# Moving the weight-side units, two banks, two loads and the weight sums of an attention + bilinear kernel

## The chip, the cores and the metric

The kernel runs on one core of one Trainium2 chip. The metric is the device time of one execution in microseconds (us): the median of three runs, which lay between 521.59 and 522.47. All numbers are float32; "hi" and "lo" below are a float32 number split into a part that the TensorE multiplies exactly (type fp32r) and its remainder.

## The reference

Per batch (8 of them) and head (8), two small attentions between 512 tokens `x` and 32 state rows; their outputs, put side by side over the heads, go through a bilinear layer:

```
scores  = x @ state.T / 8;   a  = softmax(scores)  over the 32 states;  xread = a  @ state   # 512 rows
scores2 = state @ x.T / 8;   a2 = softmax(scores2) over the 512 tokens; sread = a2 @ x       # 32 rows
X = concat(xread, sread), heads side by side           # 8 x (512 + 32) rows of 512
out = ((X @ w1) * (X @ w2)) @ w3 @ w_out               # w1, w2: 512x1024, w3: 1024x1024, w_out: 1024x512
```

## The kernel before

A prologue (to about 67 us) loads the weights, which come as float64, and computes w3 @ w_out once (`wo`, in hi and lo). Then it goes batch by batch.

*Stage 1* of a batch does not form xread. It multiplies the state of the batch into w1 and w2 (four *units* of w, `sw_steps`: each unit is 8 small matmuls, in the trace 16 instructions, of the line L147 into a two-bank PSUM tile, a copy `sw_hi` on ScalarE and a subtraction `sw_lo` on VectorE) and then multiplies the softmax `at` with the result (`stage1_sums`, L310). For each of 8 column groups `ft` this takes 12 matmuls into a two-bank tile; the two banks, one from w1 and one from w2, are multiplied on VectorE to give the hidden rows `g`.

*Stage 2* multiplies `g` with `wo`. Batches 0 and 1 do it token tile by token tile (`stage2`, L324, 24 matmuls for each of four tiles). Batches 2 to 7 (`fast_batch`) cut both operands into halves and use the scheme in which 7 products of halves stand for 8 (`stage2_quarters`, each product 24 matmuls of the line L427). It needs sums of quarters of `g` (VectorE) and sums of quarters of `wo`. The latter are made once, in batch 1, by four calls of `combine_weights`: for each, two sums, four differences and a split into `t_hi` and `t_lo`.

Called from inside stage 2 is the preparation of the next batch: its units of w (`side`), the end of its softmax (`at_hi`, `at_lo`), and the transposed `e` (L228) that 16 small DMAs move into place (`move_blocks`, L171). In the middle of stage 1, after the fourth group, PE runs `read_state` (L243), which makes sread of this batch from the tokens `x_s` and the moved `e`, and the scores of the next batch from `x_d`. After that the loads of the next tokens (`load_tokens`) and of the `x_d` after the next (`load_x`) are issued; each of these two tiles has one buffer.

Orders: PE and SP (the queue of all loads and small moves) run in the order in which the program is written. The order on ScalarE (ACT) and VectorE (DVE) is set by a scheduler. Every engine runs its queue in order. Each DMA has one of eight semaphores, and its issue waits until the previous DMA of that semaphore has landed.

PSUM: `two_banks()` takes one of three two-bank tiles in turn (`ps_2`, shown as `ps`), `bank()` one of two single banks (`ps_o`). A taker waits until the last reader of the buffer's former content is done. In `stage2_quarters` products 1 and 3 go to `bank_a`, 2 and 4 to `bank_e`, 5 and 6 to the two halves of one two-bank tile `pair`, 7 to `bank_f`; DVE adds them (L437).

Of the kernel before, what the change touches and what calls it, by code (L numbers as in the profile page):

```python
# [39 lines left out]
def attn_bilinear_kernel(  # L40
# [11 lines left out]
    B, _, NT, H, D = x_s.shape  # L52
# [35 lines left out]
    def bank():  # L88
        return ps_o.tile([P, NF], F32, name="ps_o")

    def two_banks():
        return ps_2.tile([P, 2, NF], F32, name="ps_2")
# [48 lines left out]
    def per_head(ps, b, moving):  # L141


        for j in range(NP):
            for q in range(KT):
                rows = slice(q * D, (q + 1) * D)
                nc.tensor.matmul(  # L147
                    ps[j * NS:(j + 1) * NS, q], sts[b][rows, j], moving(rows, j), start=True, stop=True
                )

    def load_x(b):
        sts[b] = att.tile([P, NP, NS], F32, name="st")
        nc.sync.dma_start(out=sts[b], in_=st[b])
        x_tiles[b] = att.tile([P, NP, S], F32, name="x_d", bufs=1)
        nc.sync.dma_start(out=x_tiles[b], in_=x_d[b])

    def load_tokens(b):
        token_tiles[b] = att.tile([P, NT, H, D], F32, name="x_s", bufs=1)
        nc.sync.dma_start(out=token_tiles[b], in_=x_s[b])
# [101 lines left out]
    def sw_pair():  # L261
        return [main.tile([P, KT, NF], F32R, name=f"sw_{part}", bufs=2 * HALF) for part in ("hi", "lo")]

    def sw_steps(b):
        sw_tiles.setdefault(b, {})

        def unit(half, i):
            ps = two_banks()
            as_q = ps.rearrange("p k (c f) -> p k c f", c=2)
            per_head(as_q, b, lambda rows, j: w_sb[rows, 2 * half:2 * half + 2, i, j])  # L270
            sw_tiles[b][half, i] = sw_pair()
            split(*sw_tiles[b][half, i], ps)

        return [(lambda half=half, i=i: unit(half, i)) for half in range(HALF) for i in range(2)]
# [66 lines left out]
    reads = {}  # L341

    def side_steps(b):


        if b == B:
            return [[reads[b - 1]], [], [], []]
        scores, reads[b], a2 = attention_steps(b)
        w = sw_steps(b)
        softmax = scores()  # L350
        first = partial(islice, softmax, 3)
        if b == 1:
            def rest():

                with tc.issue_after(stored[0].ins):
                    yield from softmax

            return [[first], [reads[0], w[0], w[1]], [], [rest], [w[2], w[3]], []]

        product = partial(islice, softmax, 1)  # L360
        return [[w[0], w[1], product, reads[b - 1], w[2], w[3], lambda: softmax], [], [], []]

    QF = FT // 2
    HT, HO = S // 2, DO // 2
# [1 line left out]
    def combine_weights(k):  # L366

        raw = [tmp_tile() for _ in range(2)]
        for i, whole in enumerate(raw):
            nc.vector.tensor_tensor(  # L370
                out=whole, in0=wo["hi"][:, i * QF + k].bitcast(F32), in1=wo["lo"][:, i * QF + k].bitcast(F32), op=ALU.add
            )
        b11, b12, b21, b22 = (whole[:, half * HO:(half + 1) * HO] for whole in raw for half in range(2))
        t = late.tile([P, QF, HO], F32, name="r22")
        for j, (x, y) in enumerate(((b12, b11), (b22, t[:, 0]), (b22, b12), (b21, t[:, 1]))):
            nc.vector.tensor_tensor(out=t[:, j], in0=x, in1=y, op=ALU.subtract)
        split(t_parts["hi"][:, :, k], t_parts["lo"][:, :, k], t)

    def tmp_tile():
        return main.tile([P, NF], F32, name="tmp", bufs=4)  # L380
# [40 lines left out]
    def product(ps, a, w, fresh):  # L421

        for k in range(QF):
            hi, lo = (t[:, k % 2] for t in a[k // 2])
            for n, (g, part) in enumerate(((hi, "lo"), (hi, "hi"), (lo, "hi"))):
                for tt in range(2):
                    nc.tensor.matmul(  # L427
                        ps[:, tt * HO:(tt + 1) * HO], g[:, tt * P:(tt + 1) * P], w(part, k),
                        start=(fresh and k == 0 and n == 0 and tt == 0), stop=(k == QF - 1 and n == 2),
                        skip_group_check=True,  # L430
                    )

    def stage2_quarters(b, q, side):
        half = lambda o: slice(o * HO, (o + 1) * HO)
        b_part = lambda i, o: (lambda part, k: wo[part][:, i * QF + k, half(o)])
        t_part = lambda j: (lambda part, k: t_parts[part][:, j, k])
        sum2 = lambda out, x, y: nc.vector.tensor_tensor(out=out, in0=x, in1=y, op=ALU.add)  # L437
        c11, c21, m7, m1 = (tmp_tile() for _ in range(4))

        def stored_quarter(o, rows, cols):  # L440
            for tt in range(2):
                first = (2 * rows + tt) * P
                nc.scalar.dma_start(out=out[b, first:first + P, half(cols)], in_=o[:, half(tt)])

        bank_a = bank()
        product(bank_a, q["a11"], b_part(0, 0), True)
        nc.scalar.copy(out=m1, in_=bank_a)
        bank_e = bank()
        product(bank_e, q["s3"], t_part(2), True)
        nc.scalar.copy(out=m7, in_=bank_e)  # L450
        a22 = quarter_pairs()
        for i in range(2):
            split(*a22[i], q["r22"][:, 2 * i:2 * i + 2])
        side()
        product(bank_a, q["a12"], b_part(1, 0), False)
        nc.scalar.copy(out=c11, in_=bank_a)
        stored_quarter(c11, 0, 0)
        s2 = quarter_pairs()
        s = [raw[:, :, 0:HT] for raw in q["raw"]]
        for i in range(2):  # L460
            split(*s2[i], s[i])
        product(bank_e, a22, t_part(3), False)
        for i in range(2):
            hi, lo = (t.bitcast(F32) for t in q["a12"][i])
            nc.vector.tensor_tensor(out=s[i], in0=hi, in1=s[i], op=ALU.subtract)
            nc.vector.tensor_tensor(out=s[i], in0=lo, in1=s[i], op=ALU.add)
        s1 = quarter_pairs()
        for i in range(2):
            split(*s1[i], q["raw"][i][:, :, HT:S])
        pair = two_banks()  # L470
        product(pair[:, 0], s2, t_part(1), True)
        sum2(m1, m1, pair[:, 0])
        sum2(c21, m1, bank_e)
        stored_quarter(c21, 1, 0)
        s4 = quarter_pairs()
        for i in range(2):
            last_split[:] = split(*s4[i], s[i])
        product(pair[:, 1], s1, t_part(0), True)
        sum2(m1, m1, pair[:, 1])
        sum2(m7, m7, m1)  # L480
        stored_quarter(m7, 1, 1)
        bank_f = bank()
        product(bank_f, s4, b_part(1, 1), True)
        sum2(m1, m1, bank_f)
        stored_quarter(m1, 0, 1)

    def fast_batch(b):
        q = {"raw": []}
        softmax = iter(())
        for ft in range(FT):  # L490
            hidden_quarters(stage1_sums(b, ft), ft, q)
            if ft == QF - 1:
                reads[b]()
                if b + 1 < B:
                    scores, reads[b + 1], _ = attention_steps(b + 1)
                    softmax = scores()
                    next(softmax)
                    load_tokens(b + 1)
                if b + 2 < B:
                    load_x(b + 2)  # L500
            elif ft in (QF, QF + 2):
                next(softmax, None)

        def side():
            if b + 1 < B:
                run(sw_steps(b + 1)[:2])
                run([lambda: softmax])
                run(sw_steps(b + 1)[2:])

        stage2_quarters(b, q, side)  # L510

    def run(steps):
        for step in steps:
            for _ in step() or ():
                pass

    def batch_stage2(b, gs):
        side = side_steps(b + 1)
        for tt in range(NT):
            stage2(gs, tt, [(out[b, tt * P:(tt + 1) * P], 0, P)])  # L520
            run(side[tt])
        if b + 1 < B:
            load_tokens(b + 1)
        if b + 2 < B:
            load_x(b + 2)


    with tc.tile_pool(name="pro", bufs=2) as pro:
# [54 lines left out]
        pair = two_banks()  # L583
# [7 lines left out]
        softmax = scores()  # L591
# [27 lines left out]
        for quarter in range(QT):  # L619
# [5 lines left out]
            if quarter == 1:  # L625
                side = side_steps(1)
# [51 lines left out]
    for b in range(1, PLAIN):  # L678
        gs = []
        for ft in range(FT):  # L680
            stage1(b, ft, gs)
            if ft % 2:
                combine_weights(ft // 2)
        batch_stage2(b, gs)
    for b in range(PLAIN, B):
        fast_batch(b)
# [46 lines left out]
```

## Time and profile before

| what | value |
|---|---|
| median of three runs | 521.85 us |
| the profiled execution: own time | 522.74 us |
| its span (first to last instruction) | 521.0 us |
| PE busy | 492.1 us, 94% |
| DVE / ACT busy | 376.6 us, 72% / 239.5 us, 46% |
| granted TensorE clock, mean | 0.99 |
| DMA | 52.48 MB, mean 101 GB/s |

PE is busy for nearly the whole span, so what can change the time is mostly where PE waits and where its clock is lowered. A row of the timeline reads: start, length, engine, line, operation, output<-inputs, shape, count, and in brackets the idle time ahead of it with what ended it. A matmul's modelled end overlaps the start of the next one; lengths of several stages are therefore best taken from start to start.

Batches in the trace: stage 1 of batch 1 runs from about 120 to 141 us, stage 2 of batch 1 from 141 to 171, and then batches 2 to 7 of about 52 us each follow (the last is shorter). The state rows (`state_rows`) are done at the end, from 483 us.

### The profile page before, as it was taken

The page shows a single profiled execution, that of the slowest core. Times are in us where ns is not written, and L with a number is a line of the kernel's source. Part 1 is how long each engine was busy: PE and PEld are TensorE (multiplying, and loading weights), DVE is VectorE, ACT ScalarE, POOL GpSimd, SP SyncE. Part 2 cuts the span into 40 slices and gives each one's busy share as a digit, 9 for nine tenths or more (in the row PEclk, how much of TensorE's full clock was granted, in tenths as well). Part 3 has the DMA queues.
Part 4 walks back from the last instruction along what each step waited for, and adds up shares of the span by engine and source line. Part 5 has one row for each costly group of instructions (what it writes and reads, how often), then busy time and mean ns, then how long its engine had stood idle before and what let it go on. Part 6 is the DMA issues. An engine that isn't in the chain of part 4 may idle for free.

```text
span 521.0 us, 8784 instructions
## 1 busy us (share of the span) xinstructions
PE 492.1 (94%) x3486; PEld 379.7 (73%) x3486; DVE 376.6 (72%) x584; ACT 239.5 (46%) x371; POOL 0.2 (0%) x4
## 2 busy tenths in 40 slices
PE   8999999999999979899989998999899989999996
PEld 5444467778858758687878786878687868899885
DVE  5769895954998369938983799379937993578780
ACT  4775973543543326504640366036503650444551
POOL 0000000000000000000000000000000000000000
PEclk9999999999999989999989999999999989999999
DMA  8996842024201334220422042203220222001101
GB/s 340 348 388 254 352 183 42 1 70 121 105 21 45 74 157 170 52 72 4 171 51 72 3 152 65 77 3 145 71 78 3 87 47 77 2 5 42 42 1 40
DMA packets 55785, 52.48 MB, mean 101 GB/s; under 512 B 42688, under 2 KB 49856, under 8 KB 51136
## 3 DMA queue, kind: packets, MB, share of 16 engines
q1 hardware_dynamic: 47488, 43.27, 25.0%
q10 hardware_dynamic: 8256, 8.65, 4.8%
q8 instruction: 27, 0.44, 0.4%
q14 instruction: 14, 0.11, 0.1%
HBM read 38.27 MB, written 8.91 MB: 91 GB/s over the span
## 4 chain that ended last, share of the span: by engine, by line
PE 69%; DVE 21%; ACT 5%; issue 4%; DMA 1%; DVEq 0%; ACTq 0%
PE ps L310 24%; PE ps_o L427 12%; PE ps_o L324 10%; PE ps L427 6%; PE ps L147 3%; DVE g_lo L98 3%; PE ps L665 3%; PE ps_o L559 3%; PE ps_o L546 3%; PE ps L546 3%; PE ps L666 1%; DVE sw_lo L98 1%; ACT e L197 1%; DVE at_lo L98 1%; DVE work L187 1%
## 5 line engine op out<-in xcount | busy, mean ns | idle before, releaser
L310 PE MATMUL ps<-at_lo,sw_hi 128*128 128x512 f32 x256 | 101.2, 395 | 0.8 <-ACT g_hi L97 0.8
L310 PE MATMUL ps<-at_hi,sw_hi 128*128 128x512 f32 x256 | 99.7, 390 | 0.0
L310 PE MATMUL ps<-at_hi,sw_lo 128*128 128x512 f32 x256 | 99.7, 389 | 0.0
L393 ACT COPY tmp<-ps 128x512 f32<-128x512 f32 x48 | 28.2, 588 | 115.1 <-PE ps L310 66.2
L310 PEld LDWEIGHTS ps<-at_lo,sw_hi 128*128 128x128 f32 x256 | 48.1, 188 | 17.8 <-DVE g_x L397 3.4
L310 PEld LDWEIGHTS ps<-at_hi,sw_lo 128*128 128x128 f32 x256 | 48.1, 188 | 10.2
L310 PEld LDWEIGHTS ps<-at_hi,sw_hi 128*128 128x128 f32 x256 | 48.1, 188 | 9.7 <-issue 0.2
L397 DVE TENSOR_TENSOR g_x<-tmp,ps 128x512 f32<-128x512 f32 x24 | 16.5, 687 | 44.1 <-ACT tmp L393 44.1
L147 PE MATMUL ps<-w_sb,st 64*32 64x512 f32 (+1 forms) x544 | 31.8, 572 | 11.8 <-DVE sw_lo L98 11.8
L97 ACT CAST g_hi<-g_x 128x512 fp32r<-128x512 f32 x48 | 29.5, 620 | 27.8 <-PE ps_o L427 13.9
L97 ACT CAST g_hi<-tmp 128x256 fp32r<-128x256 f32 (+1 forms) x54 | 27.1, 502 | 31.7 <-DVE tmp L401 16.3
L98 DVE TENSOR_TENSOR sw_lo<-ps,sw_hi 128x1024 fp32r<-128x1024 f32 (+1 forms) x34 | 38.3, 1149 | 3.9 <-ACT sw_hi L97 3.9
L97 ACT CAST sw_hi<-ps 128x1024 fp32r<-128x1024 f32 (+1 forms) x34 | 31.1, 966 | 9.3 <-PE ps L147 9.2
L98 DVE TENSOR_TENSOR g_lo<-g_x,g_hi 128x512 fp32r<-128x512 f32 x48 | 31.9, 686 | 3.1 <-ACT g_hi L97 2.0
L98 DVE TENSOR_TENSOR g_lo<-tmp,g_hi 128x256 fp32r<-128x256 f32 (+1 forms) x54 | 29.1, 540 | 4.2 <-ACT g_hi L97 3.6
L427 PE MATMUL ps_o<-wo_lo,g_hi 128*128 128x256 f32 x144 | 30.7, 296 | 0.0
L427 PE MATMUL ps_o<-wo_hi,g_lo 128*128 128x256 f32 x144 | 30.1, 292 | 0.0
L427 PE MATMUL ps_o<-wo_hi,g_hi 128*128 128x256 f32 x144 | 30.0, 291 | 0.0
L147 PEld LDWEIGHTS ps<-w_sb,st 64*32 64x32 f32 x544 | 8.2, 106 | 28.7 <-DVE sw_lo L98 17.4
L559 PE MATMUL ps_o<-w_sb,w 128*128 128x512 f32 x64 | 28.5, 599 | 0.1
L427 PEld LDWEIGHTS ps_o<-wo_lo,g_hi 128*128 128x128 f32 x144 | 24.1, 202 | 4.8 <-issue 3.5
L427 PE MATMUL ps<-t_lo,g_hi 128*128 128x256 f32 x96 | 19.8, 288 | 5.5 <-DVE tmp L437 5.5
(113 smaller groups left out, 955.1 us busy)
## 6 DMA issues: line engine op xcount, KB each, us to landing
raw<-in_w_k_dram SPq DMA_DIRECT2D x8, 1024.0 KB, 6.7
x_d<-in_x_d_dram SPq DMA_DIRECT2D x8, 1024.0 KB, 7.4
raw<-in_w_dram SPq DMA_DIRECT2D x8, 1024.0 KB, 6.3
x_s<-in_x_s_dram SPq DMA_DIRECT2D x8, 1024.0 KB, 5.1
out_dram<-tmp ACTq DMA_DIRECT2D x48, 128.0 KB, 1.9
raw<-in_w3t_dram SPq DMA_DIRECT2D x4, 1024.0 KB, 7.3
e<-work SPq DMA_DIRECT2D x96, 32.0 KB, 2.0
sread<-turned SPq DMA_DIRECT2D x128, 4.0 KB, 1.7
```

The costliest lines, as they stand in the source:

```text
L97: nc.scalar.copy(out=hi, in_=src),
L98: nc.vector.tensor_tensor(out=lo, in0=src, in1=hi.bitcast(F32), op=ALU.subtract),
L147: nc.tensor.matmul(ps[j * NS:(j + 1) * NS, q], sts[b][rows, j], moving(rows, j), start=True, stop=True)
L187: nc.vector.transpose(out=flat(s1), in_=flat(ps))
L310: nc.tensor.matmul(ps[:, i], w[:, kt, c:c + P], a[:, kt], start=(k == 0), stop=(k == 3 * KT - 1))
L324: nc.tensor.matmul(ps[:, :DO], g, wo[w][:, ft, :], start=(ft == 0 and k == 0), stop=(ft == FT - 1 and k == 2))
L393: nc.scalar.copy(out=a_sb, in_=ps[:, 0])
L397: nc.vector.tensor_tensor(out=q["raw"][p][:, kk], in0=a_sb, in1=ps[:, 1], op=ALU.mult)
L427: nc.tensor.matmul(ps[:, tt * HO:(tt + 1) * HO], g[:, tt * P:(tt + 1) * P], w(part, k), start=(fresh and k == 0 and n == 0 and tt == 0), s ...
L546: nc.tensor.matmul(w34_ps[i][:, :DO], chunks[k][:, DO + i * P:DO + (i + 1) * P], w_out[k], start=(k == 0), stop=(k == FT - 1),)
L559: nc.tensor.matmul(w34_ps[i][:, :DO], w3s[i][:, k * P:(k + 1) * P], w_out[k], start=(k == 0), stop=(k == FT - 1))
L665: nc.tensor.matmul(ps[:, i], wh[:, ks], sr[:, kt], start=(kt == 0), stop=False)
```

## The change

It has four parts.

1. In `stage2_quarters` the four units of the next batch no longer stand together behind the second product: two stand behind the first product (with the rest of the softmax), two behind the second.
2. Products 5 and 6 get tiles of their own: 5 a two-bank tile of which it uses one bank, 6 a single `bank()`.
3. In `batch_stage2`, for batch 1 (the only one that it is called for), the loads of batch 2's tokens and of batch 3's `x_d` are issued right behind batch 1's `read_state` and no longer after everything else of the stage.
4. Two of the four `combine_weights` go from stage 1 of batch 1 (after every second group) to its stage 2 (after the token tiles 1 and 2); the other two stand after the groups 3 and 7.

```diff
@@ side_steps
         product = partial(islice, softmax, 1)
-        return [[w[0], w[1], product, reads[b - 1], w[2], w[3], lambda: softmax], [], [], []]
+        loads = [partial(load_tokens, b), partial(load_x, b + 1)]
+        return [[w[0], w[1], product, reads[b - 1], *loads, w[2], w[3], lambda: softmax], [], [], []]
@@ stage2_quarters
-    def stage2_quarters(b, q, side):
+    def stage2_quarters(b, q, units):
...
         nc.scalar.copy(out=m1, in_=bank_a)
+        run(units[:3])
         bank_e = bank()
         product(bank_e, q["s3"], t_part(2), True)
...
-        side()
+        run(units[3:])
         product(bank_a, q["a12"], b_part(1, 0), False)
...
-        pair = two_banks()
-        product(pair[:, 0], s2, t_part(1), True)
-        sum2(m1, m1, pair[:, 0])
+        bank_d = two_banks()[:, 0]
+        product(bank_d, s2, t_part(1), True)
+        sum2(m1, m1, bank_d)
...
-        product(pair[:, 1], s1, t_part(0), True)
-        sum2(m1, m1, pair[:, 1])
+        bank_c = bank()
+        product(bank_c, s1, t_part(0), True)
+        sum2(m1, m1, bank_c)
@@ fast_batch
-        def side():
-            if b + 1 < B:
-                run(sw_steps(b + 1)[:2])
-                run([lambda: softmax])
-                run(sw_steps(b + 1)[2:])
-        stage2_quarters(b, q, side)
+        units = sw_steps(b + 1) if b + 1 < B else []
+        stage2_quarters(b, q, units[:2] + [lambda: softmax] + units[2:])
@@ batch_stage2
             run(side[tt])
-        if b + 1 < B:
-            load_tokens(b + 1)
-        if b + 2 < B:
-            load_x(b + 2)
+            if tt in (1, 2):
+                combine_weights(tt + 1)
@@ batch 1, stage 1
-            if ft % 2:
-                combine_weights(ft // 2)
+            if ft % 4 == 3:
+                combine_weights(ft // 4)
```

**On PE**, around the units in stage 2 of batch 4, before (a row of L147 is one unit, its 8 matmuls as built; the four `ps_` tiles are the four units; the other rows belong to products 2 and 3):

```order
L427 MATMUL ps_o<-t_hi,g_hi 128x256 x2
L427 MATMUL ps_o<-t_hi,g_lo 128x256 x2
L147 MATMUL ps_2855<-w_sb,st 32x512 x8
L147 MATMUL ps_2868<-w_sb,st 32x512 x8
L147 MATMUL ps_2906<-w_sb,st 32x512 x8
L147 MATMUL ps_2919<-w_sb,st 32x512 x8
L427 MATMUL ps_o<-wo_lo,g_hi 128x256 x2
```

After, the first pair on PE stands between products 1 and 2:

```order
L428 MATMUL ps_o<-wo_hi,g_hi 128x256 x2
L428 MATMUL ps_o<-wo_hi,g_lo 128x256 x2
L147 MATMUL ps_2823<-w_sb,st 32x512 x8
L147 MATMUL ps_2836<-w_sb,st 32x512 x8
L428 MATMUL ps_o<-t_lo,g_hi 128x256 x2
```

and the second pair on PE between products 2 and 3:

```order
L428 MATMUL ps_o<-t_hi,g_lo 128x256 x2
L147 MATMUL ps_2908<-w_sb,st 32x512 x8
L147 MATMUL ps_2921<-w_sb,st 32x512 x8
L428 MATMUL ps_o<-wo_lo,g_hi 128x256 x2
L428 MATMUL ps_o<-wo_hi,g_hi 128x256 x2
```

So product 2 (24 matmuls) now lies between the second and the third unit.

**On DVE** at the same place (batch 4), before, from the end of the softmax (L216, L221) on; `g_lo<-r` belongs to product 4, the first `g_lo<-g_x x2` to product 5, L465 and L466 prepare product 7:

```order
L412 TENSOR_TENSOR g_x<-g_x,r_2701 128x2x256
L98 TENSOR_TENSOR g_lo<-r_2701,g_hi 128x512
L413 TENSOR_TENSOR g_x<-g_x 128x2x256
L221 STREAM_TRANSPOSE work<-work 128x1024
L98 TENSOR_TENSOR g_lo<-g_x,g_hi 128x512 x2
L465 TENSOR_TENSOR g_x<-g_hi,g_x 128x2x256
L98 TENSOR_TENSOR at_lo<-work,at_hi 128x1024
L98 TENSOR_TENSOR sw_lo<-ps_2855,sw_hi 128x1024
L228 STREAM_TRANSPOSE work<-e_2715 128x1024
L98 TENSOR_TENSOR sw_lo<-ps_2868,sw_hi 128x1024
```

and on DVE after:

```order
L221 STREAM_TRANSPOSE work<-work 128x1024
L98 TENSOR_TENSOR g_lo<-tmp,g_hi 128x256
L413 TENSOR_TENSOR g_x<-g_x,r_2703 128x2x256
L98 TENSOR_TENSOR g_lo<-r_2703,g_hi 128x512
L414 TENSOR_TENSOR g_x<-g_x 128x2x256
L98 TENSOR_TENSOR at_lo<-work,at_hi 128x1024
L98 TENSOR_TENSOR sw_lo<-ps_2823,sw_hi 128x1024
L98 TENSOR_TENSOR sw_lo<-ps_2836,sw_hi 128x1024
L228 STREAM_TRANSPOSE work<-e_2717 128x1024
L98 TENSOR_TENSOR g_lo<-r_2703,g_hi 128x512
L98 TENSOR_TENSOR g_lo<-g_x,g_hi 128x512 x2
```

The transposition L221, `at_lo` and the first two `sw_lo` moved ahead of one `g_lo<-r`, both `g_lo<-g_x` and L465; nothing was added or removed.

**On SP**, in stage 2 of batch 1 (`sread` is batch 1's result on its way, `e` the 16 moves that batch 2's read waits for, `x_s` batch 2's tokens, `x_d` batch 3's), as one piece of the difference:

```order
 L171 DMA sread<-turned 32x32 x16
-L171 DMA e_1297<-work 32x8x32 x16
 L159 DMA x_s<-in_x_s_dram 128x2048
 L153 DMA st<-in_st_dram 128x128
 L155 DMA x_d<-in_x_d_dram 128x2048
+L171 DMA e_1281<-work 32x8x32 x16
 L171 DMA sread<-turned 32x32 x16
```

The three loads moved ahead of the 16 moves of `e`. In the later batches the order on SP stays.

## The prediction

> **What bounds the kernel now.** I read the page's busy times first, then the waits, then PE's timeline at each wait.
>
> ```profile
> PE 492.1 (94%) x3486; PEld 379.7 (73%) x3486; DVE 376.6 (72%) x584; ACT 239.5 (46%) x371; POOL 0.2 (0%) x4
> PE ps L147 <- DVE sw_lo L98: 11.8, 6, 2.3
> PE ps L427 <- DVE tmp L437: 5.5, 6, 1.1
> ```
>
> PE is the bound: the engine is idle for 521.0 - 492.1 = 28.9 us, and two rows of the waits (us in total, times, longest) with one wait of 4.1 in batch 2, shown further down, hold 21.4 of it. The change adds no work to PE and takes none away; it can only gain what stands in these rows, and what the clock loses beside them. The first row is a unit of w that waits for a two-bank PSUM tile until `sw_lo` of an earlier unit has read it (six times: once in batch 1, five times in stage 2 of batches 2 to 6). The second is product 6 (six times). Next, stage 2, from its first product to what follows it, as windows (length, PE busy, granted clock, DMA): batches 3, 4 and 6, the sum over batches 2 to 6, batch 7, and 3.4 us out of batch 3:
>
> ```profile
> 252.30:281.28 28.98, 25.88 (x234) 0.94 0.38 117
> 305.79:333.32 27.53, 24.39 (x234) 1.00 0.41 123
> 409.91:438.89 28.98, 25.87 (x233) 0.94 0.29 78
> sum 139.83, PE 124.92; mean PE 24.98
> 461.93:483.40 21.47, 20.38 (x169) 1.00 0.10 32
> 264.60:268.00 3.40, 3.40 (x18) 0.50 0.24 39
> ```
>
> Batches 3 and 6 are 1.45 us longer than batch 4, at a mean clock of 0.94 and not 1.00; the last row shows why: 3.4 us at half clock, which begin while the late fourth unit runs. The others have the same kind of wait without it.
>
> **Part 1 and 2, stage 2 of batches 2 to 7.** Batch 4 on PE:
>
> ```profile
> 305.79 0.40 PE L427 MATMUL ps_o<-wo_lo,g_hi 128*128 128x256 f32 x2
> 308.67 0.40 PE L427 MATMUL ps_o<-t_lo,g_hi 128*128 128x256 f32 x2
> 311.63 2.81 PE L147 MATMUL ps<-w_sb,st 64*32 64x512 f32 x48
> 316.71 1.09 PE L147 MATMUL ps<-w_sb,st 64*32 64x512 f32 x16 [2.27 <-DVE sw_lo L98]
> 327.49 0.48 PE L427 MATMUL ps<-t_lo,g_hi 128*128 128x256 f32 x2 [0.87 <-DVE tmp L437]
> ```
>
> Products 1 and 2 start 308.67 - 305.79 = 2.88 us apart: that is a product without a wait. Seven are 20.16 us, and batch 7, which has no units, takes 21.47 less its wait of 1.1, so 20.37 with the joints. An undisturbed pair of units is in batch 1:
>
> ```profile
> 146.94 1.95 PE L147 MATMUL ps<-w_sb,st 64*32 64x512 f32 x32
> 148.69 1.06 PE L147 MATMUL ps<-x_d,st 64*32 64x512 f32 x16
> 149.68 1.10 PE L243 MATMUL ps_o<-x_s,work 128*32 128x64 f32 x64
> 152.01 2.23 PE L147 MATMUL ps<-w_sb,st 64*32 64x512 f32 x32 [1.23 <-DVE sw_lo L98]
> 154.17 0.50 PE L324 MATMUL ps_o<-wo_lo,g_hi 128*128 128x512 f32 x1
> ```
>
> From start to start it is 148.69 - 146.94 = 1.75, with the return to a product some 1.85. So a stage 2 without waits is 20.37 + 2 x 1.85 = 24.07 us. The five with units sum to 139.83; 139.83 - 5 x 24.07 = 19.5 us are there to gain (waits for the tile 11.8 - 1.2 = 10.6, product 6 5.5 - 1.1 = 4.4, half clock 2 x 1.45 = 2.9, the rest restarts after waits), and 1.1 in batch 7.
>
> Do the waits go? It is DVE that sets them, so I follow DVE and ACT in batch 4 with the new order:
>
> ```profile
> 308.29 0.41 DVE L402 TENSOR_TENSOR r<-tmp,ps 128x256 f32<-128x256 f32 x1
> 311.36 1.24 DVE L221 STREAM_TRANSPOSE work<-work 128x1024 f32<-128x1024 f32 x1
> 314.30 1.22 DVE L98 TENSOR_TENSOR at_lo<-work,at_hi 128x1024 fp32r<-128x1024 f32 x1
> 316.56 1.24 DVE L228 STREAM_TRANSPOSE work<-e 128x1024 f32<-128x1024 f32 x1
> 323.49 1.90 DVE L98 TENSOR_TENSOR g_lo<-g_x,g_hi 128x512 fp32r<-128x512 f32 x3
> 327.38 0.69 DVE L437 TENSOR_TENSOR tmp<-tmp,ps_o 128x512 f32<-128x512 f32 x1
> 312.64 1.05 ACT L97 CAST at_hi<-work 128x1024 fp32r<-128x1024 f32 x1
> 313.59 2.84 ACT L97 CAST sw_hi<-ps 128x1024 fp32r<-128x1024 f32 x3
> ```
>
> DVE runs without a pause from before 308 to 325.4. Up to L402 (done at 308.6) the orders agree. `at_lo` and a `sw_lo` take 316.56 - 314.30 = 2.26 together, 1.13 each. Of the 2.74 us that then stood ahead of L221, one `g_lo<-r` of 0.6 is moved back; L221 (1.15) comes first. So `at_lo` starts at 308.6 + 1.15 + 2.14 = 311.9, the first `sw_lo` ends at 311.9 + 1.13 + 1.13 = 314.2, the second at 315.3. ACT does not hold it up: `at_hi` (1.05) can start with the end of L221 at 309.8, and the two `sw_hi` behind it take 0.95 each, the first done near 311.9. PE: product 1 to 308.7, units 1 and 2 to 310.5, product 2 to 313.4, unit 3 to 314.3 in the third tile, and unit 4 wants the first tile back at 314.3, as the first `sw_lo` ends at 314.2. The wait of 2.27 us is gone, with nothing to spare. Products 3, 4 and 5 would start at 315.2, 318.1 and 321.0; the `g_lo<-r` that was moved back ends at 317.1, needed at 319.5; both `g_lo<-g_x` at 318.2, needed at 321.0. Product 6 (323.9) no longer waits for the sum over product 5, since `bank_c` was left by ACT's copy of `c11` after product 3. Product 7 (326.8) needs `bank_e` back from the second L437; behind the row at 323.49, which ends where it did (325.4), two of them of 0.7 end at 326.8. Again nothing to spare. Then DVE, not PE's tile, ends these stages, within tenths; I take 0.2 us off the gain in each of batches 3 to 6 (batch 2's DVE runs over a microsecond earlier): 19.5 - 0.8 = 18.7. Bounds: no residue, 19.5; one more 1024-wide operation (1.13) in the way in each of the five, 19.5 - 5.7 = 13.8. I stay near the first, as the walk has every row. The half clock I count as gone because it came where the unit was late; without a wait of 2 us there is none in the windows.
>
> **Part 4, the sums of wo, and the second pair in batch 1.** Ahead of batch 1's units on DVE stood two whole `combine_weights`, the last of which ended with the `t_lo` below; now one does:
>
> ```profile
> 149.60 1.23 DVE L98 TENSOR_TENSOR t_lo<-r,t_hi 128x1024 fp32r<-128x1024 f32 x1 [1.11 <-ACT t_hi L97]
> 150.74 2.35 DVE L98 TENSOR_TENSOR sw_lo<-ps,sw_hi 128x1024 fp32r<-128x1024 f32 x2
> 166.95 1.24 DVE L228 STREAM_TRANSPOSE work<-e 128x1024 f32<-128x1024 f32 x1
> ```
>
> The last `t_lo` now ends near 147.7, so `sw_lo` starts as soon as PE and ACT have given it a unit, at 149.0 and not 150.74. The tile is free at 150.2, before the read ends at 150.7; the pair follows at once: 154.17 - 149.68 = 4.49 becomes 1.0 + 1.85, a gain of 1.6 (bounds 0 and 1.6). The two sums that moved stand among the softmax of batch 2: one addition ahead of L221 (as wide as an L437, so 0.6 to 0.7), and some 1.3 that run while DVE would wait for `at_hi`. Starting 1.7 earlier, `at_lo` still ends before 167; PE wants it at 169.2, when the token tiles are done. The rest runs behind L228, where DVE then had nothing to do until batch 2's first group. They hide.
>
> **Part 3, the loads.** Batch 2's read against batch 4's, then SP and landing times:
>
> ```profile
> 181.27 0.39 PE L310 MATMUL ps<-at_hi,sw_lo 128*128 128x512 f32 x1
> 185.74 2.48 PE L243 MATMUL ps_o<-x_s,e 128*32 128x64 f32 x64 [4.08 <-issue]
> 189.92 0.50 PE L310 MATMUL ps<-at_lo,sw_hi 128*128 128x512 f32 x1
> 291.96 0.39 PE L310 MATMUL ps<-at_hi,sw_lo 128*128 128x512 f32 x1
> 294.33 0.50 PE L310 MATMUL ps<-at_lo,sw_hi 128*128 128x512 f32 x1
> 155.80 10.06 SPq L171 DMA_DIRECT2D sread<-turned  x16
> 168.25 11.49 SPq L171 DMA_DIRECT2D e<-work  x16
> 179.84 0.54 SPq L159 DMA_DIRECT2D x_s<-in_x_s_dram  x1
> x_s<-in_x_s_dram SPq DMA_DIRECT2D x1, 1024.0 KB, 5.7
> x_d<-in_x_d_dram SPq DMA_DIRECT2D x1, 1024.0 KB, 7.3
> ```
>
> The tokens are issued at 179.84, behind 16 moves of 11.5 us, land 5.7 later and release the read at 185.74; the stretch around the read is 8.65 us where it is 2.37 in batch 4, partly because after 4 us of idling its small matmuls take 2.48 and not 1.1. At most 6.28 to gain. The `sread` moves start at 155.80 on a transposition by DVE that now comes 1.7 earlier with all of DVE's queue; so they go from 154.1 to 164.1, the loads to 165.6; tokens land near 170, `x_d` near 173. `e` is moved from 167.2 (L228 ends a microsecond earlier), one per 0.65 to 0.7, each waiting for its semaphore's former transfer: the fifth for the tokens, about when it would issue anyway, the eighth for the first move, which may sit behind `x_d` until 172.5. The last lands near 180. PE comes at 181.5 - 1.6 = 179.9. So the read waits tenths: I take 0.4, gain 5.9 (bounds 0 and 6.28). One output store of ACT shares a semaphore with `x_d` and holds ACT until about 173.5, a group late; PE has three tiles, and the fourth group needs the first back only at 177.5.
>
> **Sum.** 18.7 + 1.1 + 1.6 + 5.9 = 27.3 us. Against the profiled execution (522.74: the span of 521.0 and 1.74 around it) that is 495.4. The median of the runs shown is 0.89 lower, so I forecast 521.85 - 27.3 = 494.5 us.
>
> **Rivals.** (a) The half clock stays. The Trainium skill ("TensorE: Matmul & The Clock Gate", Why this matters for your kernels) asks for no idle gap above about 3 us; by that rule waits of 2.3 us would not have lowered the clock and their end would not raise it. Here two of the five stages with such a wait (at most 2.3 us) lose clock, and both right at the wait, which speaks for the wait; against it speaks that three did not. If something else in the stage lowers it, the two stretches of 1.45 stay: 497.4. (b) DVE is the new bound: the walk leaves no slack at unit 4 and product 7, and one 1024-wide operation more in the way per batch brings 500.2 - 0.8 = 499.4. (c) The read gains nothing: the `e` moves stall behind the two megabytes. For it speaks that `x_d` lands 7.3 after its issue; against, that most of the 16 moves issue after 170 in any case. 494.5 + 5.9 = 500.4. The skill's page "DMA: Bandwidth & Descriptors" (Queues, rings and completion order) says that descriptors on an engine are consumed in ring order, so a move waits for the loads ahead of it; by that rule the moves issued before 172.5 land then, and no later ones are held. (d) Slower: the splits of products 4, 5 and 7, now behind `at_lo`, two `sw_lo` and L228 (4 x 1.13 = 4.5 us), come late in every batch. It decides when DVE ends over 5.5 us per batch later than the walk says (27.3 / 5); the whole displaced work is 4.5, and half of it stood ahead of them before. Priced at 6 us a batch: 521.85 + 2.7 = 524.6.
>
> **Chances.** My walk 0.70, (a) 0.10, (b) 0.10, (c) 0.06, (d) 0.03, no effect at all 0.01. Range: low from gains without any residue (27.3 + 0.8 + 0.4 = 28.5, so 493.3) and 0.3 a batch for joints that may close further, 491.8; high 499.6, which takes in (a) and (b) and leaves out (c). A measurement here can tell some 0.2%, 1 us: faster 0.95, within it 0.02, slower 0.03.
>
> **What would show it.** Right: no row of PE's L147 or L427 waiting over 0.3 us in batches 3 to 6, stage 2 windows of 24 to 24.4 us at clock 1.00, batch 2's read within 1 us of the group before it, 154.17 come down to about 152.6. Wrong: L147 still released by `sw_lo`, product 7 by L437, products 4 or 5 by `g_lo`, or half clock in any stage 2.

## The result, and the profile after

The changed kernel takes 496.74 us (median of four runs, 496.68 to 497.24) against 521.76 (521.59 to 522.47) for the kernel before on the same chip: a ratio of 0.952, 95% interval 0.9504 to 0.9537. The forecast was 494.5 us, with a range of 491.8 to 499.6.

The profiled execution has an own time of 496.68 us and a span of 494.9. The page's busy line, and then all rows that the view of PE's waits lists (us in total, times, longest):

```profile
PE 486.4 (98%) x3486; PEld 376.0 (76%) x3486; DVE 375.3 (76%) x584; ACT 238.8 (48%) x371; POOL 0.2 (0%) x4
PE ps_o L542 <- DVE w_sb L134: 1.1, 1, 1.1
PE ps_o L77 <- DVE work L74: 1.0, 1, 1.0
PE ps_o L243 <- DMA e<-work: 0.8, 1, 0.8
PE ps L310 <- ACT g_hi L97: 0.8, 4, 0.2
PE ps_o L428 <- DVE tmp L438: 0.5, 1, 0.5
```

Neither the row of L147 (11.8 us before) nor the 5.5 us of product 6 is left; the first two rows belong to the start of the kernel. PE's busy time fell by 5.7 us too, although it does the same instructions: at half clock and after waits the same matmuls take longer (the 64 of a read took 2.48 us in batch 2, mostly at half clock, and 1.10 in batch 4). The stages, as windows (length, PE busy with its count, and the granted clock as the number ahead of the last two): stage 2 of batches 2 and 4, the sum over batches 2 to 6, batch 7, the second pair of units in batch 1, and batch 2's read:

```profile
193.90:218.18 24.28, 24.28 (x233) 21.24 (x232) 22.01 (x33) 11.92 (x18) 0.00 (x0) 1.00 0.46 139
291.50:315.78 24.28, 24.28 (x233) 21.23 (x232) 22.26 (x33) 11.99 (x18) 0.00 (x0) 1.00 0.46 140
sum 121.40, PE 121.40 PEld 106.18 DVE 110.78 ACT 59.88 POOL 0.00; mean PE 24.28 PEld 21.24 DVE 22.16 ACT 11.98 POOL 0.00
436.42:457.34 20.92, 20.37 (x169) 20.19 (x168) 16.26 (x26) 10.26 (x18) 0.00 (x0) 1.00 0.08 27
149.34:152.28 2.94, 2.94 (x105) 1.31 (x97) 2.94 (x4) 1.10 (x2) 0.00 (x0) 1.00 0.04 8
179.40:182.88 3.48, 2.63 (x82) 1.25 (x80) 2.29 (x5) 1.82 (x3) 0.00 (x0) 1.00 0.12 19
```

In stage 2 PE is busy for 24.28 of 24.28 us at full clock. From start to start, before and after:

| stretch | before | after | gain | forecast |
|---|---|---|---|---|
| stage 2 of batches 2 to 6 | 139.83 | 121.40 | 18.43 | 18.7 |
| batch 2's read | 8.65 | 3.48 | 5.17 | 5.9 |
| second pair in batch 1 | 4.49 | 2.94 | 1.55 | 1.6 |
| stage 2 of batch 7 | 21.47 | 20.92 | 0.55 | 1.1 |
| start of the kernel, to 119.65 / 119.31 | | | 0.34 | 0 |
| sum, against 521.0 - 494.9 = 26.1 | | | 26.04 | 27.3 |

### The profile page after: what moved, and what is told of

The parts are those of the page before. It is cut to its first block, busy times and chain, and to the rows that moved or that the text cites. A ratio compares the mean times of both kernels' runs of the same rounds, so it can differ in the third digit from the quotient of the medians.

```text
span 494.9 us, 8790 instructions
## 1 busy us (share of the span) xinstructions
PE 486.4 (98%) x3486; PEld 376.0 (76%) x3486; DVE 375.3 (76%) x584; ACT 238.8 (48%) x371; POOL 0.2 (0%) x4
## 3 DMA queue, kind: packets, MB, share of 16 engines
q10 hardware_dynamic: 8256, 8.65, 5.0%
## 4 chain that ended last, share of the span: by engine, by line
PE 83%; DVE 9%; DMA 3%; ACT 2%; issue 1%; SPq 1%; ACTq 0%; DVEq 0%
PE ps L310 29%; PE ps_o L428 20%; PE ps_o L324 8%; PE ps L147 6%; PE ps_o L555 6%; PE ps L661 3%; PE ps L428 3%; PE ps_o L542 3%; PE ps L542 3%; DMA e<-work 2%; PE ps L662 2%; DVE work L187 1%; DVE m L204 1%; DVE m L190 1%; SPq L171 1%
## 5 line engine op out<-in xcount | busy, mean ns | idle before, releaser
L147 PE MATMUL ps<-w_sb,st 64*32 64x512 f32 (+1 forms) x544 | 31.4, 570 | 0.0
L428 PE MATMUL ps_o<-wo_lo,g_hi 128*128 128x256 f32 x144 | 29.6, 287 | 0.5 <-DVE tmp L438 0.5
L428 PE MATMUL ps_o<-t_lo,g_hi 128*128 128x256 f32 x144 | 29.5, 287 | 0.0
L428 PE MATMUL ps_o<-t_hi,g_hi 128*128 128x256 f32 x144 | 29.0, 283 | 0.0
L428 PE MATMUL ps_o<-wo_hi,g_hi 128*128 128x256 f32 x144 | 29.0, 283 | 0.0
L428 PE MATMUL ps_o<-wo_hi,g_lo 128*128 128x256 f32 x144 | 29.0, 283 | 0.0
L428 PE MATMUL ps_o<-t_hi,g_lo 128*128 128x256 f32 x144 | 29.0, 283 | 0.0
```

What stands on the lines that cost most here:

```text
L147: nc.tensor.matmul(ps[j * NS:(j + 1) * NS, q], sts[b][rows, j], moving(rows, j), start=True, stop=True)
L428: nc.tensor.matmul(ps[:, tt * HO:(tt + 1) * HO], g[:, tt * P:(tt + 1) * P], w(part, k), start=(fresh and k == 0 and n == 0 and tt == 0), s ...
```

## Experiments

**Each part alone.** The first four runs put one part of the change into the kernel before. They share 15 runs of that kernel (522.67 us).

*Part 1, the units in two pairs.*

```diff
         nc.scalar.copy(out=m1, in_=bank_a)
+        run(units[:3])
         bank_e = bank()
...
-        side()
+        run(units[3:])
```

> The kernel before with part 1 alone (units of w in two pairs). Theory (each part takes its own wait): stage 2 of batches 2 to 6 loses the wait of unit 4 and its half clock, but keeps product 6's wait of some 0.9 us: about 25.2 us each, 126 in place of 139.8, so 508 us. Rival (DVE is the bound, the units' place is not): the wait turns up at products 5 to 7, stage 2 stays above 27 us, 518 us or more.

515.44 us (515.16 to 516.42), ratio 0.9866 (0.9838 to 0.9893): a gain of 7.2 and not 14. Its waits of PE, the row of product 6 in batch 3, the DVE sum that ended it, and stage 2 of batch 3:

```profile
PE ps L427 <- DVE tmp L437: 9.5, 6, 2.0
PE ps L147 <- DVE sw_lo L98: 1.2, 1, 1.2
271.63 0.48 PE L427 MATMUL ps<-t_lo,g_hi 128*128 128x256 f32 x2 [1.61 <-DVE tmp L437]
270.81 0.68 DVE L437 TENSOR_TENSOR tmp<-tmp,ps 128x512 f32<-128x512 f32 x1
251.34:277.46 26.12, 24.51 (x234) 21.29 (x232) 22.14 (x33) 11.99 (x18) 0.00 (x0) 1.00 0.42 130
```

The units no longer wait in stage 2 (the 1.2 us left are batch 1's). But product 6 waits 9.5 us in all where it waited 5.5. Once PE arrives some 2 us earlier, DVE is late with the sum over product 5, which product 6 waits for since both use the same two-bank tile. So theory and rival are each right in part: the wait at the unit is gone, as the theory has it, and four tenths of it (4.0 of 10.6 us) come back at product 6, as the rival has it.

*Part 2, tiles of their own for products 5 and 6.*

```diff
-        pair = two_banks()
-        product(pair[:, 0], s2, t_part(1), True)
+        bank_d = two_banks()[:, 0]
+        product(bank_d, s2, t_part(1), True)
...
-        product(pair[:, 1], s1, t_part(0), True)
+        bank_c = bank()
+        product(bank_c, s1, t_part(0), True)
```

> The kernel before with part 2 alone (products 5 and 6 in separate tiles). Theory: product 6's waits (5.5 us in all) go, the late fourth unit stays with its 2.3 us in each of batches 2 to 6: 516.5 us, give or take 1.45 for each stretch of half clock more or fewer than before's. Rival (the sums over the products are late on DVE anyway, so that the wait goes on to product 7): under 1 us of gain, 521 us.

515.43 us (514.38 to 515.92), ratio 0.9859 (0.9831 to 0.9888). Product 6's waits are gone; what is left of the line is 0.7 us in batch 7:

```profile
PE ps L147 <- DVE sw_lo L98: 11.8, 6, 2.3
PE ps_o L427 <- DVE tmp L437: 0.7, 1, 0.7
251.63:279.62 27.99, 25.73 (x234) 21.92 (x232) 22.47 (x33) 12.18 (x18) 0.00 (x0) 0.94 0.39 121
304.13:330.56 26.43, 24.16 (x234) 21.18 (x232) 22.27 (x33) 12.19 (x18) 0.00 (x0) 1.00 0.42 128
```

The late unit stays as it was, and with it a stretch of half clock in batch 3. At full clock a stage takes 27.53 us before, 26.1 with part 1, 26.4 with part 2 and 24.28 with both (in the changed kernel, beside parts 3 and 4; the two without those were not run): gains of 1.4, 1.1 and 3.25. The two belong together; each alone leaves PE at the other's wait.

*Part 3, the loads behind batch 1's read.*

```diff
-        return [[w[0], w[1], product, reads[b - 1], w[2], w[3], lambda: softmax], [], [], []]
+        loads = [partial(load_tokens, b), partial(load_x, b + 1)]
+        return [[w[0], w[1], product, reads[b - 1], *loads, w[2], w[3], lambda: softmax], [], [], []]
...
-        if b + 1 < B:
-            load_tokens(b + 1)
-        if b + 2 < B:
-            load_x(b + 2)
```

> The kernel before with part 3 alone (batch 2's loads behind batch 1's read). Theory: batch 2's read goes from 8.65 to about 3.5 us as in the changed kernel, since the moves of e and PE both come 1.5 us later than there: 516.7 us. Rival (the loads must come early enough, which needs the sums moved as well, or else the moves of e behind them hold the read): the read stays above 6 us, 519.5 us or more.

518.95 us (517.55 to 520.48), ratio 0.9928 (0.9902 to 0.9955): 3.7 us, between the two. The read is no longer released by the tokens but by the last moves of `e`, and waits half as long (0.85 us in the changed kernel, where part 4 stands beside it):

```profile
184.05 1.05 PE L243 MATMUL ps_o<-x_s,e 128*32 128x64 f32 x58 [2.13 <-DMA e<-work]
```

*Part 4, the sums of wo spread.*

```diff
-            if ft % 2:
-                combine_weights(ft // 2)
+            if ft % 4 == 3:
+                combine_weights(ft // 4)
...
             run(side[tt])
+            if tt in (1, 2):
+                combine_weights(tt + 1)
```

> The kernel before with part 4 alone (sums of wo spread). Theory: the second pair of units in batch 1 comes 1.55 us earlier, and all of DVE's queue with it, so that batch 2's loads come over a microsecond earlier too: 520.5 us. Rival (the loads do not move, since they stand behind the moves of e): what the pair gains is waited for at batch 2's read, 521.8 us.

520.94 us (520.38 to 522.12), ratio 0.9971 (0.9957 to 0.9985): 1.7 us, as the theory had it. The pair in batch 1 no longer waits, and batch 2's read still waits for its loads, but less than the 4.08 us before:

```profile
183.15 2.51 PE L243 MATMUL ps_o<-x_s,e 128*32 128x64 f32 x64 [3.34 <-issue]
```

The four gains are 7.2 + 7.2 + 3.7 + 1.7 = 19.8 us of 25 to 26. The rest exists only where the parts meet: (3.25 - 1.4 - 1.1) x 5 = 3.7 us in stage 2, and the half clock, of which every part alone left at least one stretch in the middle of its profile.

**Part 1 undone in the changed kernel** (parts 2, 3, 4 kept, all four units behind product 2 again).

```diff
-        run(units[:3])
...
-        run(units[3:])
+        side()
```

> The changed kernel with part 1 undone (units of w together again behind product 2; parts 2, 3, 4 kept). Theory (the fourth unit's wait for its tile is what part 1 removed, and part 2 does not touch it): stage 2 of batches 2 to 6 goes from 24.28 to some 26.4 us as with part 2 alone, plus 1.45 for one or two stretches of half clock: 496.7 + 10.5 + 2 = 509 us, half clock at the late unit in some batches. Rival (part 2 alone would do, once DVE is ahead by parts 3 and 4): stage 2 below 25 us, 500 us or less.

509.48 us (506.5 to 509.77), ratio to before 0.9729 (0.9687 to 0.9771), as the theory had it. The unit waits again, and two of the five stages (batches 3 and 4) have half clock; of the others batch 5 is shown:

```profile
PE ps L147 <- DVE sw_lo L98: 10.6, 5, 2.3
244.76:272.69 27.93, 25.66 (x233) 22.68 (x232) 22.50 (x33) 12.18 (x18) 0.00 (x0) 0.94 0.39 121
349.72:376.12 26.40, 24.17 (x234) 21.18 (x232) 22.24 (x33) 12.20 (x18) 0.00 (x0) 1.00 0.42 128
```

Of its four runs three had a mean clock of 0.992 to 0.993 and took 509.4 to 509.8 us; the fourth had 0.999 and took 506.5. The 3 us between them fit two stretches of half clock that this run did not have, though its instructions are the same; no profile shows that run, so this is inferred from its mean clock.

**The clock by itself.** The kernel before, with ten matmuls by zeros ahead of the fourth unit. They add nothing to product 1's bank and fill the time in which PE stands.

```diff
+    FILL = 10
...
-                run(sw_steps(b + 1)[2:])
+                run(sw_steps(b + 1)[2:3])
+                for _ in range(FILL):
+                    nc.tensor.matmul(side.bank[:32, :HO], zero, wo["hi"][:, 0, :HO], start=False, stop=True,
+                                     skip_group_check=True)
+                run(sw_steps(b + 1)[3:])
```

> The kernel before with ten products by zeros (added to the bank of product 1, which they leave as it is) between the third and the fourth unit, in the time in which PE waits there. Theory (half clock follows a stretch of 3.41 us in which PE is busy for less than some 1.5): no stage 2 has half clock, all five take 27.5 us or a tenth more, in every run; 520 us and no run above 522. Rival (the units themselves, which keep little of PE busy, lower the clock): one to three stages of 29 us as before.

520.15 us (519.04 to 521.71) against 522.54, ratio 0.9955 (0.994 to 0.997). Work for nothing made the kernel 0.45% faster. The only half clock left between 100 and 490 us in its profile is at batch 2's read, where nothing was filled in. Batches 3 and 6, which have half clock in the profile of before, and the sum of all five (139.83 before):

```profile
253.12:280.59 27.47, 25.65 (x244) 22.21 (x242) 22.32 (x33) 12.10 (x18) 0.00 (x0) 1.00 0.40 123
409.21:436.69 27.48, 25.66 (x244) 22.21 (x242) 22.33 (x33) 12.10 (x18) 0.00 (x0) 1.00 0.30 82
sum 136.78, PE 128.32 PEld 111.10 DVE 111.60 ACT 60.32 POOL 0.00; mean PE 25.66 PEld 22.22 DVE 22.32 ACT 12.06 POOL 0.00
```

**The two waits that the change left.** First product 7's bank taken from the two-bank tiles:

```diff
-        bank_f = bank()
+        bank_f = two_banks()[:, 0]
```

> The changed kernel with product 7's bank from the three two-bank tiles in place of the one that product 4 and the sum behind it hold. Theory (batch 7's wait of 0.55 us is for that bank alone): the wait goes, 496.2 us. Rival (what comes behind it waits for the same late sums, the tail above all): 496.7 us, no change.

496.54 us (496.29 to 496.94); in its profile batch 7's stage 2 takes 20.15 us with no wait. That alone does not show that the bank did it, as the next two runs tell. Second, batch 2's loads ahead of the `sread` moves, by a step inside `read_state`:

```diff
-        def read_state():
+        def read_state(loads=()):
...
+            run(loads)
             scaled = att.tile([P, KT, D], F32, name="scaled")
...
-        return [[w[0], w[1], product, reads[b - 1], *loads, w[2], w[3], lambda: softmax], [], [], []]
+        return [[w[0], w[1], product, partial(reads[b - 1], loads), w[2], w[3], lambda: softmax], [], [], []]
```

> The changed kernel with batch 2's loads issued right behind the matmuls of batch 1's read, ahead of the sread moves. Theory (two moves of e were held by the loads and made the last one late): loads land before 162, no move of e is held, batch 2's read takes 2.4 and not 3.5 us: 495.7 us. Rival (the loads hold the sread moves on SP instead, and those the moves of e): the read waits as before or longer, 496.7 us or more.

495.91 us (495.82 to 497.47). The read waits for nothing (SP's queue, then PE's row):

```profile
152.02 1.51 SPq L155 DMA_DIRECT2D x_d<-in_x_d_dram  x1
154.52 11.44 SPq L171 DMA_DIRECT2D sread<-turned  x16
167.49 11.06 SPq L171 DMA_DIRECT2D e<-work  x16
180.36 1.10 PE L243 MATMUL ps_o<-x_s,e 128*32 128x64 f32 x64
```

In the changed kernel the 16 moves of `e` took 12.58 us and here 11.06; the `sread` moves took 11.44 and not 10.05, for which PE does not wait. But batch 7's wait is gone in this profile too, although its bank is the old one. Third, that wait's other suspect: batch 7's output DMAs issued by SP, so that ACT does not stand at their semaphores.

```diff
-                nc.scalar.dma_start(out=out[b, first:first + P, half(cols)], in_=o[:, half(tt)])
+                queue = nc.sync if b == B - 1 else nc.scalar
+                queue.dma_start(out=out[b, first:first + P, half(cols)], in_=o[:, half(tt)])
```

> The changed kernel with batch 7's output issued by SP and not by ACT. Theory (product 7 of batch 7 waits 0.55 us since ACT stood 2.3 us at an output DMA's semaphore and DVE's split came late by it): the wait goes, 496.2 us. Rival (it waits for DVE's own queue): the wait stays, 496.7 us.

496.65 us (496.24 to 497.2), beside 496.41 for the changed kernel: no gain that can be told, though the wait is gone. ACT in the changed kernel, and batch 7 with SP issuing:

```profile
446.20 2.27 ACTq L444 DMA_DIRECT2D out_dram<-tmp  x2
437.36:457.51 20.15, 20.15 (x169) 20.14 (x168) 16.36 (x26) 10.35 (x18) 0.00 (x0) 1.00 0.09 28
```

The wait belongs to ACT's 2.27 us: in a second profile of the changed kernel these two DMAs took 2.41 us and the wait was 0.7, while in the kernel with the loads first they took 0.82 us, and the old bank did no harm. Why ACT's DMAs stood in some programs and not in others was not tried; the bank's own part stays open, since in its run they took 0.82 us as well.

Both edits together, alone and then beside the changed kernel on one chip:

> Both of the former two edits. Theory: they add up, since they lie 270 us apart: 495.1 us. Rival: only one of them gains, 495.7 to 496.2 us.

> The changed kernel once more, as the measure for the next three on the same chip: 496.7 us, no half clock between 100 and 490 us.

> Loads first and product 7's own bank once more, now beside the changed kernel. Theory: 1.4 us less from batch 1's stage 1 on (the profiles of both show 371.53 and 370.13 us), so 495.3 us against 496.7. Rival (the difference lies in the start of the kernel, which varies by a microsecond): no difference.

495.79 us (495.29 to 496.47) in the first: the new bank adds nothing that can be told to the loads alone (495.91), as the rival had it. In the second it is 495.63 (495.34 to 495.89) against 496.41 (496.29 to 498.24) for the changed kernel. So both edits gain about 0.8 us, 0.16%, with ranges that do not touch: less than the 1.4 us that the profiles gave, and at the edge of what a measurement here tells. In the trace of the second the removed pause at the read (1.1 us) is partly paid back: from the end of the read to stage 2 of batch 2 PE needs 12.5 us and not 12.0, with one more wait of 0.2 for ACT's `g_hi`. This version is the fastest of those that ran. The changed kernel came out at 0.9517 (0.9498 to 0.9536) of before this time.

## Why the prediction was right, and where it was off

The four parts gained by the mechanisms that were forecast; the sum came 2.24 us low, for reasons that follow term by term.

**Parts 1 and 2.** The walk held. In batch 4 the two units of the first pair and of the second, product 7, and DVE's rows that had to be in time:

```profile
294.46 1.95 PE L147 MATMUL ps<-w_sb,st 64*32 64x512 f32 x32
299.40 1.95 PE L147 MATMUL ps<-w_sb,st 64*32 64x512 f32 x32
312.90 0.40 PE L428 MATMUL ps_o<-wo_lo,g_hi 128*128 128x256 f32 x2
298.73 2.34 DVE L98 TENSOR_TENSOR sw_lo<-ps,sw_hi 128x1024 fp32r<-128x1024 f32 x2
311.94 0.69 DVE L438 TENSOR_TENSOR tmp<-tmp,ps_o 128x512 f32<-128x512 f32 x1
```

By the traces, what removes the wait at the fourth unit is the order on DVE. PE reaches that unit 8.65 us into the stage before (314.44, where the row at 311.63 ends) and 8.85 after, hardly later; but the first `sw_lo` ends 8.4 us into the stage and no longer 10.8 (316.56, where L228 follows it), since L221, `at_lo` and `sw_lo` now stand ahead of splits that stood ahead of them. Moving the units on PE and the order on DVE came in one edit; neither was tried without the other.

The first `sw_lo` ends half way through its row, at 299.9; unit 4, half way through the second pair, starts near 300.4. The sum over product 4 ends at 312.6 and product 7 starts at 312.9. "Nothing to spare" at both places was right; the slack is some 0.3 to 0.5 us, and the 0.2 us per batch that I took off were not lost. What I missed is the price of a pair: 20.15 us for seven products (batch 7 without its wait) and 24.28 with two pairs make (24.28 - 20.15) / 2 = 2.07 each, and not 1.85. My 20.37 for seven products held 0.2 us of restart after batch 7's wait. So the stage is 24.28 and not 24.07; 5 x 0.21 = 1.05 us too little, 0.8 taken off for nothing: 18.43 against 18.7. That the two errors nearly cancel is luck.

**The half clock** went, as forecast, and not by rival (a): no stage 2 is below full clock. The Trainium skill's rule that I weighed against it ("TensorE: Matmul & The Clock Gate", Why this matters for your kernels: no idle gaps above about 3 us) is too wide a limit here: waits of at most 2.3 us brought half clock in two of five stages before, and filling them took it away.

**Part 3** was the largest miss in a term: 5.17 us and not 5.9. The read waits 0.85 us where I took 0.4, and stopping costs some 0.3 us more (the stretch takes 3.48 us, in batch 4 before 2.37). I had the mechanism but not its size:

```profile
164.06 0.54 SPq L159 DMA_DIRECT2D x_s<-in_x_s_dram  x1
166.88 12.58 SPq L171 DMA_DIRECT2D e<-work  x16
180.88 1.05 PE L243 MATMUL ps_o<-x_s,e 128*32 128x64 f32 x58 [0.85 <-DMA e<-work]
```

The first move of `e` landed 6.7 us after its issue, at 173.6, just behind `x_d` (173.2), and the eighth move had to wait for that semaphore until then, a microsecond later than I had assumed. What I missed is an output store of ACT: issued at 164.88, it landed only at 172.28, and the seventh move waited 1.4 us for its semaphore. That DMA engines consume descriptors in ring order is what the Trainium skill says in "DMA: Bandwidth & Descriptors" (Queues, rings and completion order), and the trace agrees for the move behind the loads on SP's queue. The store is on ACT's queue; what slowed it was not tried. Rival (c) was thus right by 0.7 of its 5.9 us; with the loads first it is gone. The wait is not always 0.85: in three more profiles with the loads where the changed kernel has them (the new bank, the output by SP, and the changed kernel once more) it is 1.1, 1.1 and 1.6 us.

The prediction put the slow read of before (2.48 us) down to 4 us of idling. It was the clock: a third stretch of half clock begins within it, beside the two that the prediction counted. In the part 3 kernel 58 of the 64 matmuls took 1.05 us at full clock right after a wait of 2.13.

```profile
186.12:189.53 3.41, 3.29 (x78) 2.04 (x76) 1.11 (x3) 0.00 (x0) 0.00 (x0) 0.50 0.34 142
```

**Part 4 and the second pair in batch 1**: 1.55 us against 1.6, and the sums that moved cost nothing that shows.

**Batch 7**: product 6's wait of 1.1 us went, and product 7 got one of 0.55, which the prediction lists among the signs of being wrong ("product 7 by L437", now L438). ACT's output DMAs, whose queue the walk did not follow in this batch, set it.

**Rival (b)**, DVE as the new bound, is wrong for the change as a whole and comes true in part with part 1 alone, where product 6 waits 9.5 us for a sum on DVE. **Rival (d)** did not come: L147, products 4, 5 and 6 wait for nothing.

**The base.** The terms give 26.04 of 27.3 us; that is 1.26 of the 2.24 by which I was low. The other 1.0 came from subtracting them from the median of three runs and not from the profiled execution (522.74 - 26.06 = 496.68). The later medians of the kernel before, 522.67, 522.33 and 522.54 over 37 runs, lie nearer to the profiled time than those three runs did.

## What to carry to other kernels

Two waits in a row on one engine are one chain: cost an edit that removes the first by what the second then waits for, and plan both edits together. Where halves of one PSUM tile go to different products, as here, the second waits for the reader of the first (5.5 us in six stages). Price a step with its joints from a stage without waits, look at the queues of every engine in the one stage that differs (here the last batch), and subtract terms of a trace from the time of that trace.

## What the runs showed of the hardware

The stretches of half clock follow a grid. In the profile of before they start at 186.12, 264.63 and 421.64 us, which are 23 and 46 steps of 3.413 apart. Here are the windows of that length (the second number is PE's busy time) just before a stretch began: the three of before, then the highest one of the part 1 kernel and that of the kernel with zeros.

```profile
182.71:186.12 3.41, 0.38 (x5) 0.32 (x6) 1.69 (x3) 1.24 (x2) 0.00 (x0) 1.00 1.01 408
261.22:264.63 3.41, 1.46 (x19) 0.62 (x20) 3.41 (x4) 1.93 (x3) 0.00 (x0) 1.00 0.00 0
418.23:421.64 3.41, 1.18 (x24) 0.18 (x16) 3.41 (x4) 2.28 (x3) 0.00 (x0) 1.00 0.00 0
320.38:323.79 3.41, 1.38 (x12) 1.21 (x11) 2.58 (x4) 0.77 (x2) 0.00 (x0) 1.00 0.41 87
180.81:184.22 3.41, 1.45 (x7) 0.87 (x5) 1.29 (x3) 1.11 (x2) 0.00 (x0) 1.00 0.74 223
```

And windows on the grid after which the clock stayed full: the lowest of before, of the part 3 kernel and of the part 4 kernel.

```profile
366.99:370.40 3.41, 1.65 (x21) 0.81 (x22) 3.41 (x4) 1.93 (x3) 0.00 (x0) 1.00 0.00 0
257.06:260.47 3.41, 1.60 (x32) 0.31 (x16) 3.41 (x5) 3.41 (x4) 0.00 (x0) 1.00 0.15 60
259.02:262.43 3.41, 1.60 (x20) 0.77 (x21) 3.41 (x4) 1.93 (x3) 0.00 (x0) 1.00 0.00 0
```

All 15 stretches between 100 and 490 us in the profiles of this study follow a window with 1.46 us or less of PE work, and no window at full clock with 1.60 or more was followed by one. So in these profiles it is not the length of a gap that counts but how much of one such window PE worked (by its busy time, whose ends are modelled), with the limit between 43 and 47%. The same wait of 2.3 us lowers the clock or not by how it falls on the grid, which explains two of five in the profile of before and fits the varying times of kernels that have such waits. That the window is free-running and 3413 ns long stands in the Trainium skill ("TensorE: Matmul & The Clock Gate", What's actually happening); the trace agrees. A stretch lasted a second window where the first, at half clock, was not full of work:

```profile
183.85:187.26 3.41, 2.56 (x72) 2.28 (x80) 0.44 (x2) 0.25 (x1) 0.00 (x0) 0.50 0.71 296
187.26:190.68 3.42, 3.42 (x20) 1.47 (x21) 2.37 (x5) 0.00 (x0) 0.00 (x0) 0.50 0.02 2
```

These are from the kernel with part 1 alone. Three of the 15 stretches were so long, with 2.56, 2.16 and 1.63 us of work in the first window; the other twelve, with 3.2 us or more, ended after one.
